# A gated linear attention feeding a SiLU feed-forward: the second token group by plain products, no gap between attention chunks, and an audit held in its written order

## The chip, the core and the metric

The kernel runs on one core of a Trainium2 chip. The core has TensorE (PE: matrix products and transposes, results in PSUM), VectorE (DVE: elementwise work, scans, reductions), ScalarE (ACT: copies out of PSUM, Silu), GpSimd (POOL) and SyncE (SP), whose queue issues all the transfers of this kernel. Each engine works through its own instructions in order; semaphores let one engine wait for another. The metric is the device time of one execution in microseconds; the times below are the median of repeated runs, and the profile is of one execution of its own.

## What is computed

The first part is a recurrent attention with a decay per key channel, for 4 sequences, 8 heads, 768 steps and 48 channels. The second part is a feed-forward network over the 3072 resulting tokens of 384 features, with 2048 hidden features.

```python
# attention, q, k, v, alpha: (4, 8, 768, 48)
for t in range(S):
    state = alpha[:, :, t, :, None] * state + einsum('bhd,bhe->bhde', k[:, :, t], v[:, :, t])
    y[:, :, t] = einsum('bhd,bhde->bhe', q[:, :, t], state)
x = y.transpose(0, 2, 1, 3).reshape(B * S, H * D)      # (3072, 384)
h = x @ w_in                                            # (384, 2048)
out = (h * sigmoid(h)) @ w_out                          # (2048, 384)
```

The inputs reach the kernel as 64-bit floats (the weights) or 32-bit floats; all arithmetic on the chip is in float32.

## The kernel before, in words

**Two paths.** The function `quotients` computes the fast path. It divides by running products of `alpha`, which is only sound if `alpha` and the weights lie in certain bounds, so it also checks its inputs (`audit`, line 576) and hands back a flag. Where the flag says no, `general` computes everything again; on these inputs that branch isn't taken.

**Attention** is cut into 24 chunks of 128 tokens, numbered n, and each goes through four stages:
- `products(n)` (line 612): twelve transposes on PE, a copy on ACT, then on DVE a scan (625), a product (629), a small maximum and a reciprocal (631, 632), a second scan (634) and a product (636).
- `scores(n)` (638): sixteen short matmul records, two masks on DVE (651), four transposes and a copy; for chunks past the first four a decay of the state on DVE (660).
- `values(n)` (665): 32 or 56 narrow matmul records and a copy that lays two chunks side by side as `xt`.
- `states(n)` (686): the state's update, on PE and DVE (699 or 701).

**Feed-forward** works on groups of 512 tokens, four chunks each; there are six groups. Each has two halves h of 256 tokens. It is cut into small "pieces", Python generators that yield after a few instructions.
- `enter_plain(grp, h)` (727) multiplies by w_in plainly: for each pair of the 16 hidden tiles, six products into one PSUM bank, then one Silu. Only group 0 uses it.
- `enter(grp, pair)` (743) computes the same for both halves and half the hidden tiles (a "pair" of "quads" of tiles) by a scheme with fewer products: 20 products for 24, twice, with many additions on DVE (line 770) and copies on ACT (762). It needs eleven sums of tokens (`sums_x`, 709) and 23 sums of w_in blocks (`sums_w`, 531, the list `SUMS_W`), some in place in `w_in`, some in the tile `wx`.
- `leave(grp, h)` (850) multiplies by w_out, in seven steps of eight products of 192 columns (857), with differences of w_out blocks (`t1`, `t2`, `t4` in the tile `wt`, and `b12` in place, `differences`, 539), subtractions between cells of the hidden activations (862) and sums of cells (`side_by_side`, 842). The first one, `leave(0, 0)`, is plain: 64 records of 384 columns (884). Between its four pieces it issues the differences and the first twelve w_in sums; `leave(0, 1)` issues the rest.
- The weights arrive as 64-bit floats. `weights` (544) fetches a block (461, four buffers `bits`) and converts it with one ACT and three DVE instructions (564, 567 to 569): twelve blocks of w_in, sixteen of w_out.

**The order.** Everything is traced in one program order, from which the compiler's scheduler makes the order of each engine: it prefers what was traced first, but lets an instruction go ahead where it expects it to be ready. `tc.keep_in_program_order(i)` pins an instruction behind the one traced before it on the same engine. The loop at line 1022 runs over steps; each step has four slots (`scores` of the chunk before, `products`, `values`, `states`), and behind each slot `fill` (998) adds feed-forward pieces. `begin` (991) leaves two steps without a new chunk after the fourth one. A list `pieces` (968) holds the order: group 0 plain, `leave(0, 0)`, `leave(0, 1)`, `sums_x(1)`, `enter(1, 0)`, `enter(1, 1)`, and from then on `leave(g-1, h)` and `enter(g, h)` alternately (`both`, 960). `fill` deals them out in even shares per slot; `last` keeps a piece back until its chunks are bridged (`values` done). `convert` (953) runs the weight conversions ahead of the pieces that need them.

**The audit.** From step 15 on, every second slot calls `audit` once: it issues a transfer of a piece of `alpha`, w_in or w_out into one buffer and, at once, one or two reductions of it on DVE (602). There are 37 pieces with 65 reductions; those that don't fit into the loop follow in the tail (1035), two feed-forward pieces to each. The flag is computed from them at the end.

**PSUM**: three banks for attention (`ps_a`), three for the products with w_in (`ps_m`), two for those with w_out (`ps_o`). The hidden activations live in six buffers (`gpool`).

Of the kernel before, what the change touches and what calls it, by code (L numbers as in the profile page):

```python
# [355 lines left out]
def quotients(  # L356
# [31 lines left out]
    GB = 4  # L388
# [132 lines left out]
    def combine(to, sa, a, sb, b):  # L521
        if sa == sb == 1:
            dve.tensor_tensor(to, a, b, ALU.add)
        elif sa == 1:
            dve.tensor_tensor(to, a, b, ALU.subtract)
        elif sb == 1:
            dve.tensor_tensor(to, b, a, ALU.subtract)
        else:
            dve.scalar_tensor_tensor(to, a, -1.0, b, ALU.mult, ALU.subtract)

    def sums_w(upto):
        while sums_done[0] < min(upto, len(SUMS_W)):
            to, sa, a, sb, b = SUMS_W[sums_done[0]]
            combine(block_w(to), sa, block_w(a), sb, block_w(b))
            sums_done[0] += 1

    sums_done = [0]

    def differences(i):
        dve.tensor_tensor(t1[:, i], b12[:, i], b11[:, i], ALU.subtract)  # L540
        dve.tensor_tensor(t2[:, i], b22[:, i], t1[:, i], ALU.subtract)
        dve.tensor_tensor(t4[:, i], b21[:, i], t2[:, i], ALU.subtract)
# [33 lines left out]
    def audit():  # L576
# [13 lines left out]
        for src, n, kind in todo:  # L590
            t = late["look"].tile([128, 512, 2], I32, name="bits")
            if kind == 0:
                x = t.rearrange("p n w -> p (n w)")[:, 0:n].bitcast(F32)
                nc.sync.dma_start(x, src)
            else:
                nc.sync.dma_start(t[:, 0:n, :].rearrange("p n w -> p (n w)"), src.bitcast(I32))
                x = t[:, 0:n, 1]
            i = at[kind]
            at[kind] += 1
            for which, op in ((0, ALU.max), (1, ALU.min)):  # L600
                if kind == 1 or which == 0:
                    dve.tensor_reduce(seen[kind][which][:, i : i + 1], x, axis=AX, op=op,  # L602
                                      apply_absolute_value=True)
            yield
# [122 lines left out]
    def enter_plain(grp, h):  # L727

        if h == 0:
            for pair in range(NQ // 2):  # L730
                g_tiles(grp, pair)
        xt = xts[2 * grp + h]
        for f in range(0, NFT, 2):
# [6 lines left out]
            act.activation(gts[grp, h, q // 2][:, i : i + 2, q % 2, :], ps, AF.Silu)  # L740
# [109 lines left out]
    def leave(grp, h):  # L850
# [24 lines left out]
        if grp == h == 0:  # L875
# [3 lines left out]
            for j in range(HF // 2):  # L879
# [16 lines left out]
            for i in range(0, HF, 2):  # L896
                dve.tensor_tensor(b12[:, i : i + 2], b22[:, i : i + 2], b12[:, i : i + 2], ALU.subtract)
# [6 lines left out]
        def done():  # L904
            if grp == 0:
                sums_w(12 + 2 * next(steps) + 2)
# [53 lines left out]
    def both(grp):  # L960
        last = GB * grp + GB
        pieces.append((sums_x(grp), last))
        for h in range(2):
            x, y = leave(grp - 1, h), enter(grp, h)
            for _ in range(7):
                pieces.extend(((x, last), (y, last)))

    pieces = []
    for part, n, last in ((enter_plain(0, 0), HF, 2), (enter_plain(0, 1), HF, 4),
                          (leave(0, 0), HF // 2, 4), (leave(0, 1), 7, 4),  # L970
                          (sums_x(1), 1, 2 * GB), (enter(1, 0), 7, 2 * GB), (enter(1, 1), 7, 2 * GB)):
        pieces += [(part, last)] * n
    ALONE = 15
    START = len(pieces) - ALONE
    for grp in range(2, NG):
        both(grp)
    for h in range(2):
        pieces += [(leave(NG - 1, h), NT)] * 7
# [14 lines left out]
    FIRST = 4  # L993
    SLOTS = 4

    STEADY = (begin[2 * GB - 1] + 1) * SLOTS + 3

    def fill(step, slot):

        if step < FIRST:  # L1000
# [115 lines left out]
```

## Time and profile before

| | us |
|---|---|
| median of three runs (618.08 to 619.08) | 618.42 |
| the profiled execution | 622.89 |
| its span, first to last instruction | 621.1 |
| PE busy | 585.3 |
| PE weight load busy | 521.4 |
| DVE busy | 435.0 |
| ACT busy | 184.7 |
| mean granted TensorE clock | 0.98 of full speed |

A page of the profile lists busy time by engine, the span in 40 equal slices, the transfers, the chain of work that ended last, and the costliest groups of instructions. These are the slices: each digit is the busy share in tenths, and PEclk is the granted clock.

```profile
PE   4889989998999979999999999999999999999996
PEld 3668876697777869989978999999999999999996
DVE  3897999868978798677689577479377365444531
ACT  1335441010335434134233224224233233242200
```

A row of a group of instructions reads: line, engine, operation, output <- input, shape, count | busy time and mean ns of one | idle time of the engine just before them, and what ended it. A row of a stretch gives its bounds and length, then the busy time and the number of instructions of each engine. A row of the timeline gives start, duration, the instruction, and in brackets the idle time before it with its releaser. A row of the chain gives start, duration and the instructions. Busy times of PE overlap, since matmuls are pipelined.

### The profile page before, as it was taken

How to read it: one execution, taken by the hardware profiler on the slowest of the kernel's cores; microseconds unless marked ns; L12 is line 12 of the kernel's file. 1: busy time of each engine (PE TensorE's matmuls, PEld its weight loads, DVE VectorE, ACT ScalarE, POOL GpSimd, SP SyncE). 2: the span in 40 equal slices, each digit the busy share in tenths (PEclk: the TensorE clock that was granted, in tenths of full speed). 3: DMA queues.
4: the chain of work that ended last, by engine and by line, in shares of the span. 5: the costliest groups of instructions: out<-in, count | busy, mean ns of one | idle time of the engine just before them, and what ended most of it. 6: DMA issues, size and time to landing. Idle time of an engine off the chain costs nothing.

```text
span 621.1 us, 10850 instructions
## 1 busy us (share of the span) xinstructions
PE 585.3 (94%) x4450; PEld 521.4 (84%) x4450; DVE 435.0 (70%) x802; ACT 184.7 (30%) x311; POOL 5.2 (1%) x22
## 2 busy tenths in 40 slices
PE   4889989998999979999999999999999999999996
PEld 3668876697777869989978999999999999999996
DVE  3897999868978798677689577479377365444531
ACT  1335441010335434134233224224233233242200
POOL 3000000000000000000000000000000000000000
PEclk9789999997999989999998999999999999999999
DMA  9986964165664524445353233033010000000000
GB/s 208 222 173 199 249 145 86 33 152 155 171 154 85 141 59 92 137 105 115 103 133 72 71 58 52 20 55 55 20 34 1 14 14 6 20 7 13 15 20 30
DMA packets 116169, 54.25 MB, mean 87 GB/s; under 512 B 101648, under 2 KB 107792, under 8 KB 116112
## 3 DMA queue, kind: packets, MB, share of 16 engines
q1 hardware_dynamic: 116112, 53.49, 37.7%
q8 instruction: 36, 0.59, 0.4%
q14 instruction: 21, 0.17, 0.1%
HBM read 48.76 MB, written 4.72 MB: 86 GB/s over the span
## 4 chain that ended last, share of the span: by engine, by line
PE 56%; DVE 27%; DMA 12%; issue 2%; ACT 1%; POOL 1%; DVEq 0%; ACTq 0%; SPq 0%; POOLq 0%
PE ps_o L857 27%; PE ps_m L756 19%; DMA bits<-in_moe_w_out_dram 5%; DMA bits<-in_moe_w_in_dram 5%; DVE seen L602 5%; PE ps_a L680 3%; PE ps_a L620 3%; DVE g L770 3%; DVE p L634 2%; DVE u L625 2%; DMA bits<-in_alpha_dram 2%; PE ps_a L647 2%; DVE u L629 1%; DVE p L636 1%; PE ps_a L655 1%
## 5 line engine op out<-in xcount | busy, mean ns | idle before, releaser
L857 PE MATMUL ps_o<-w_out,g 128*128 128x192 f32 x704 | 126.8, 335 | 0.6 <-DVE o L871 0.6
L857 PEld LDWEIGHTS ps_o<-w_out,g 128*128 128x128 f32 x704 | 118.9, 196 | 3.8 <-issue 1.4
L857 PE MATMUL ps_o<-wt,g 128*128 128x192 f32 x528 | 91.8, 327 | 0.0
L756 PE MATMUL ps_m<-xc,w_in 128*128 128x256 f32 x360 | 88.1, 380 | 1.0 <-DVE g L770 0.9
L857 PEld LDWEIGHTS ps_o<-wt,g 128*128 128x128 f32 x528 | 86.3, 190 | 1.5 <-issue 0.8
L756 PEld LDWEIGHTS ps_m<-xc,w_in 128*128 128x128 f32 x360 | 66.9, 190 | 9.6 <-DVE g L770 1.5
L602 DVE TENSOR_REDUCE seen<-bits 128x1 f32<-128x384 int32 (+2 forms) x65 | 43.2, 689 | 36.9 <-DMA bits<-in_moe_w_out_dram 16.1
L762 ACT COPY g<-ps_m 128x512 f32<-128x512 f32 x80 | 46.8, 588 | 70.2 <-PE ps_m L756 70.2
L767 ACT ACTIVATE g<-g 128x1024 f32<-128x1024 f32 x40 | 41.2, 1054 | 74.1 <-DVE g L770 74.1
L756 PE MATMUL ps_m<-xc,wx 128*128 128x256 f32 x240 | 62.2, 381 | 0.0
L862 DVE TENSOR_TENSOR g<-g 128x512 f32<-128x512 f32 x66 | 45.1, 687 | 17.0 <-PE ps_o L857 16.9
L770 DVE TENSOR_TENSOR g<-ps_m,g 128x512 f32<-128x512 f32 x70 | 46.9, 684 | 6.9 <-PE ps_m L756 5.7
L756 PEld LDWEIGHTS ps_m<-xc,wx 128*128 128x128 f32 x240 | 43.6, 190 | 5.1 <-issue 1.0
L737 PE MATMUL ps_m<-xt,w_in 128*128 128x256 f32 x192 | 45.5, 391 | 0.5 <-DVE w_in L569 0.5
L647 PE MATMUL ps_a<-p,u 48*128 48x128 f32 x384 | 30.2, 297 | 12.5 <-DVE p L636 11.8
L647 PEld LDWEIGHTS ps_a<-p,u 48*128 48x128 f32 x384 | 25.4, 198 | 19.5 <-issue 14.0
L737 PEld LDWEIGHTS ps_m<-xt,w_in 128*128 128x128 f32 x192 | 36.4, 196 | 6.2 <-DVE w_in L569 1.0
L651 DVE TENSOR_TENSOR g<-ps_a,mask 128x512 f32<-128x512 f32 x48 | 31.6, 686 | 11.6 <-PE ps_a L647 11.2
L762 ACT COPY part<-ps_m 128x512 f32<-128x512 f32 x40 | 23.5, 587 | 52.8 <-PE ps_m L756 34.6
L625 DVE TENSOR_TENSOR_SCAN u<-al,one 128x516 f32<-128x516 f32 x24 | 29.5, 1229 | 10.9 <-ACT al L622 10.8
L770 DVE TENSOR_TENSOR g<-g,part 128x512 f32<-128x512 f32 x30 | 20.5, 683 | 17.8 <-ACT part L762 12.8
L756 PE MATMUL ps_m<-xt,w_in 128*128 128x256 f32 x120 | 31.0, 381 | 0.7 <-DVE g L770 0.7
(102 smaller groups left out, 658.4 us busy)
## 6 DMA issues: line engine op xcount, KB each, us to landing
bits<-in_moe_w_in_dram SPq DMA_DIRECT2D x24, 512.0 KB, 3.8
bits<-in_moe_w_out_dram SPq DMA_DIRECT2D x32, 384.0 KB, 3.5
an<-in_alpha_dram SPq DMA_DIRECT2D x24, 192.0 KB, 4.0
kn<-in_k_dram SPq DMA_DIRECT2D x24, 192.0 KB, 4.7
qn<-in_q_dram SPq DMA_DIRECT2D x24, 192.0 KB, 4.7
vn<-in_v_dram SPq DMA_DIRECT2D x24, 192.0 KB, 3.7
bits<-in_alpha_dram SPq DMA_DIRECT2D x9, 512.0 KB, 3.9
out_dram<-o SPq DMA_DIRECT2D x48, 96.0 KB, 1.6
```

The lines of the kernel that those rows point to most:

```text
L602: dve.tensor_reduce(seen[kind][which][:, i : i + 1], x, axis=AX, op=op, apply_absolute_value=True)
L620: pe.transpose(ps[name][:, j, :], c[name][:, 2 * j : 2 * j + 2, :], ident)
L625: dve.tensor_tensor_scan(u[:, end - 1 :: -1], sg[:, end:0:-1], one[:, end:0:-1], 0.0, ALU.mult, ALU.add)
L647: pe.matmul(ps[u][:, j, :], lhsT=c["kp"][r, j, :], rhs=c["qp"][r, j, :], start=True, stop=True)
L651: dve.tensor_tensor(g[:, u], ps[u], mask[:, None, :].to_broadcast([128, NP, C]), ALU.mult)
L737: pe.matmul(ps[:, e, :], lhsT=w_in[:, t, (f + e) * 128 : (f + e + 1) * 128], rhs=xt[:, t, :], start=(t == 0), stop=(t == NKT - 1))
L756: pe.matmul(ps[:, e], lhsT=block_w(w)[:, 2 * pair + e], rhs=block_x(grp, x), start=(first and e == 0), stop=(e == 1), skip_group_check=True)
L762: act.copy(to, ps)
L767: act.activation(x, x, AF.Silu)
L770: dve.tensor_tensor(to, a, b, op)
L857: pe.matmul(ps, lhsT=x, rhs=w[:, i], start=(first and i == 0), stop=(i == HF - 1), skip_group_check=True)
L862: dve.tensor_tensor(cells(grp, h, pair, *to), cells(grp, h, pair, *x), cells(grp, h, pair, *y), ALU.subtract)
```

## The change

Group 1 goes through `enter_plain` too, so `enter`, `sums_x` and the w_in sums start with group 2. `enter_plain` now takes one pair (half the hidden tiles) at a time. The differences, `side_by_side(0, 1, ...)` and `b12` move out of `leave(0, 0)` into the plain pieces of group 1's first pair. `sums_w` works on one pair of quads, so each sum becomes two of half the width: those of the first pair are issued in `leave(0, 1)`, which now alternates with group 1's second pair, those of the second in `leave(1, 0)`, four to a step; they are pinned in program order, as is the first of each set of differences. `begin` and its gap go. The pieces carry weights (`n`), and `fill` deals them out by phases that end at given slots. The conversions are spread anew. In `audit` the generator now yields between a transfer and its reductions, so a call runs the reductions of the piece before and then issues the next transfer, and the reductions are pinned in program order.

```diff
+    def sums_w(pair, upto):
+        r = slice(2 * pair, 2 * pair + 2)
+        while sums_done[pair] < min(upto, len(SUMS_W)):
+            to, sa, a, sb, b = SUMS_W[sums_done[pair]]
+            tc.keep_in_program_order(
+                combine(block_w(to)[:, r], sa, block_w(a)[:, r], sb, block_w(b)[:, r]))
+            sums_done[pair] += 1
...
+    def differences(i):
+        if i < HF // 2:
+            i = slice(2 * i, 2 * i + 2)
+            tc.keep_in_program_order(
+                dve.tensor_tensor(t1[:, i], b12[:, i], b11[:, i], ALU.subtract))
+            dve.tensor_tensor(t2[:, i], b22[:, i], t1[:, i], ALU.subtract)
+            dve.tensor_tensor(t4[:, i], b21[:, i], t2[:, i], ALU.subtract)
         else:
...
+            i -= HF // 2
+            if i % 2 == 0:
+                side_by_side(0, 1, i // 2)
+            i = slice(2 * i, 2 * i + 2)
+            dve.tensor_tensor(b12[:, i], b22[:, i], b12[:, i], ALU.subtract)
...
+            yield
             i = at[kind]
             at[kind] += 1
             for which, op in ((0, ALU.max), (1, ALU.min)):
                 if kind == 1 or which == 0:
...
+                    tc.keep_in_program_order(
+                        dve.tensor_reduce(seen[kind][which][:, i : i + 1], x, axis=AX, op=op,
+                                          apply_absolute_value=True))
...
-    def enter_plain(grp, h):
+    def enter_plain(grp, h, pair):
...
+            if grp == 1 and pair == 0:
+                differences(4 * h + f // 2)
+            if grp > 0 and f % 8 == 6:
+                side_by_side(grp, h, pair)
             yield
...
-                differences(slice(2 * j, 2 * j + 2))
-                if j % 2 == 1:
-                    side_by_side(0, 1, j // 2)
-                sums_w(3 * j + 3)
...
         def done():
-            if grp == 0:
-                sums_w(12 + 2 * next(steps) + 2)
+            if 2 * grp + h in (1, 2):
+                sums_w(2 * grp + h - 1, 4 * next(steps) + 4)
...
+    for h in range(2):
+        for pair in range(2):
+            pieces += [plain(0, h, pair)] * 4
+    pieces += [(leave(0, 0), 24, GB)] * (HF // 2)
+    phases = [len(pieces)]
+    for h in range(2):
+        pieces += [plain(1, h, 0)] * 4
+    both([(leave(0, 1), 12, GB)] * 7, [plain(1, 0, 1)] * 4 + [plain(1, 1, 1)] * 4)
+    phases.append(len(pieces))
+    before = output(1)
     for grp in range(2, NG):
...
+        pieces.append((sums_x(grp), 0, GB * grp + GB))
+        for x, y in zip(before, group(grp)):
+            both(x, y)
+        phases.append(len(pieces))
+        before = output(grp)
+    pieces += before[0] + before[1]
...
-    begin = [n if n < GB else n + 2 for n in range(NT)]
-    STEPS = begin[-1] + 2
...
+    marks = [2 * SLOTS + 2] + [(GB * i + 2 * GB) * SLOTS + 2 for i in range(len(phases))]
...
+        due = a + (b - a) * (at - marks[i] + 1) / (marks[i + 1] - marks[i])
+        if i >= 2 and at % 2:
+            next(audits, None)
+        while work_at[done + 1] <= due and pieces[done][2] <= bridged:
             convert(0, 3 * (done // 2) + 6)
-            convert(1, 2 * done - 8)
+            convert(1, 3 * (done - 6) // 2)
```

By this order `leave(0, 0)` begins at step 6 and ends in step 8, group 1's plain pieces run from there to step 12, and the audit's first call comes at the end of step 12.

More of the change, by code (lines that the diff above doesn't have):

```diff
@@ L725, in bank @@
         return banks[turn[i]].tile([128, 512], F32, name="ps_m")[:, 0:n]
-    def enter_plain(grp, h):
+    def enter_plain(grp, h, pair):
         if h == 0:
-            for pair in range(NQ // 2):
-                g_tiles(grp, pair)
+            g_tiles(grp, pair)
         xt = xts[2 * grp + h]
-        for f in range(0, NFT, 2):
+        for f in range(8 * pair, 8 * pair + 8, 2):
             ps = bank(f // 2 % 3).rearrange("p (e n) -> p e n", e=2)
@@ L1024, in quotients @@
                 ((scores, 1), (products, 0), (values, 1), (states, 1))):
-            if step - lag in begin:
-                n = begin.index(step - lag)
+            n = step - lag
+            if 0 <= n < NT:
                 stage(n)
```

78 lines of the change are left out of this document (26 added, 52 removed).

## The prediction

> **What bounds the kernel now.** I read the page's busy rows first, then the busy time by stretch, then the same stretches for single lines of TensorE (PE) work, then the chain that ended last, then the timeline where PE waits.
>
> ```profile
> span 621.1 us, 10850 instructions
> PE 585.3 (94%) x4450; PEld 521.4 (84%) x4450; DVE 435.0 (70%) x802; ACT 184.7 (30%) x311; POOL 5.2 (1%) x22
> ```
> ```profile
> 0.00:60.00 60.00, 45.85 (x362) 37.02 (x363) 43.89 (x79) 19.63 (x32) 5.16 (x22) 0.91 0.97 200
> 60.00:123.00 63.00, 59.89 (x387) 45.13 (x386) 60.89 (x121) 18.09 (x35) 0.00 (x0) 1.00 0.52 127
> 123.00:227.00 104.00, 93.72 (x869) 81.59 (x869) 83.86 (x144) 32.44 (x55) 0.00 (x0) 0.97 0.58 141
> 227.00:340.00 113.00, 110.19 (x846) 100.66 (x848) 89.67 (x173) 35.29 (x61) 0.00 (x0) 0.97 0.45 104
> ...
> 340.00:616.00 276.00, 275.64 (x1998) 257.00 (x1990) 156.71 (x288) 79.26 (x130) 0.00 (x0) 1.00 0.13 28
> 616.00:621.10 5.10, 0.00 (x0) 0.00 (x0) 0.03 (x1) 0.00 (x0) 0.00 (x0) 0.86 0.09 26
> ```
>
> Columns of a stretch: its length, busy time of PE, PE weight load, VectorE (DVE), ScalarE (ACT), GpSimd, then granted clock, DMA share, GB/s. PE looks 94% busy, but matmuls overlap, so a busy row hides idle time. I count work instead: records times their spacing where PE never waits.
>
> ```profile
> 344.33 2.59 PE ps_m L756 x12
> ...
> 579.17 36.48 PE ps_o L857 x224
> ```
>
> The same stretches for one line of PE work each; first line 756, then 857, 884 and 737 (PE busy and records, weight load):
>
> ```profile
> 123.00:227.00 104.00, 38.11 (x160) 28.95 (x160) 0.97 0.58 141
> ...
> 340.00:616.00 276.00, 105.29 (x456) 85.07 (x456) 1.00 0.13 28
> ```
> ```profile
> 123.00:227.00 104.00, 21.02 (x112) 19.64 (x113) 0.97 0.58 141
> ...
> 340.00:616.00 276.00, 148.25 (x864) 141.33 (x864) 1.00 0.13 28
> ```
> ```profile
> 60.00:123.00 63.00, 21.21 (x64) 11.85 (x64) 1.00 0.52 127
> ```
> ```profile
> 0.00:60.00 60.00, 18.78 (x74) 14.67 (x75) 0.91 0.97 200
> ```
>
> The chain gives 2.59/12 = 0.2158 us per 256-wide record and 36.48/224 = 0.1629 per 192-wide one. Every product leaves two records, a transpose one. Of the 1998 records in 340-616 lines 756 and 857 have 456 and 864, so the other 678 (attention) take (275.64 - 456 x 0.2158 - 864 x 0.1629)/678 = 0.054 each. Line 884's 64 take 21.2; line 737 has 74 of its 192 before 60 and 118 after; line 756 has 800 in all and 857 has 1232, so what 123-227 and 340-616 don't hold of them lies in 227-340. Work and idle by stretch:
> - 0-60: 74 x 0.2158 + 288 x 0.054 = 31.5; idle 28.5.
> - 60-123: 118 x 0.2158 + 21.2 + 205 x 0.054 = 57.7; idle 5.3.
> - 123-227: 160 x 0.2158 + 112 x 0.1629 + 597 x 0.054 = 85.0; idle 19.
> - 227-340: 184 x 0.2158 + 256 x 0.1629 + 406 x 0.054 = 103.3; idle 9.7.
> - 340-616: idle about 0; after it a tail of 5.1.
>
> So PE bounds the kernel from 227, and about 53 us are lost before. To 123 the cover is DVE, 60.89 busy of 63. In 123-227 DVE is neither full nor fast:
>
> ```profile
> 125.12 1.22 DVE L602 TENSOR_REDUCE seen<-bits 128x1 f32<-128x1024 f32 x1 [2.84 <-DMA bits<-in_alpha_dram]
> ...
> 137.01 1.22 DVE L602 TENSOR_REDUCE seen<-bits 128x1 f32<-128x1024 f32 x1 [2.30 <-DMA bits<-in_alpha_dram]
> ...
> 141.91 2.08 PE L647 MATMUL ps_a<-p,u 48*128 48x128 f32 x16 [2.24 <-DVE p L636]
> ```
> ```profile
> L602 DVE TENSOR_REDUCE seen<-bits 128x1 f32<-128x512 int32 (+1 forms) x25 | 21.4, 873 | 17.1 <-DMA bits<-in_moe_w_in_dram 9.5 <-DMA bits<-in_alpha_dram 7.7
> ```
>
> The audit's reduces, written after step 15, were issued from 120 on. DVE sat 2.84 us for one's transfer, attention's scan came late behind it, and PE waited 2.24. Up to 227 the audit took 21.4 us of DVE and left 17.1 idle.
>
> A sentence on a page of the Trainium skill, which nothing below needs: "Perfetto Trace Analysis", Identifying the Most-Contended Engine, calls matmul busy time a bad measure of headroom and weight-load busy time a good one. By the busy rows only 27.5 us are idle to 227; by weight load, full at 257.0/276 = 0.931, 163.7/0.931 leaves 51, and my count says 53, so the trace sides with the page.
>
> **The change part by part.** PE: group 1 takes 96 plain products for 80, two records each: 32 x 0.2158 = **+6.9 us**, surely on the path. DVE:
>
> ```profile
> L770 DVE TENSOR_TENSOR g<-ps_m,g 128x512 f32<-128x512 f32 x70 | 46.9, 684 | 6.9 <-PE ps_m L756 5.7
> ...
> L523 DVE TENSOR_TENSOR xc<-xt 128x256 f32<-128x256 f32 x15 | 6.1, 418 | 0.1
> ...
> L523 DVE TENSOR_TENSOR w_in<-wx,w_in 128x512 f32<-128x512 f32 x4 | 2.6, 682 | 0.0
> ...
> L540 DVE TENSOR_TENSOR wt<-w_out 128x384 f32<-128x384 f32 x4 | 2.2, 546 | 0.0
> ```
> ```profile
> L625 DVE TENSOR_TENSOR_SCAN u<-al,one 128x516 f32<-128x516 f32 x24 | 29.5, 1229 | 10.9 <-ACT al L622 10.8
> L634 DVE TENSOR_TENSOR_SCAN p<-al,inv 128x516 f32<-128x516 f32 x24 | 29.5, 1228 | 0.2
> ...
> L629 DVE TENSOR_TENSOR u<-ps_a,u 128x512 f32<-128x512 f32 x24 | 16.6, 690 | 1.8
> L636 DVE TENSOR_TENSOR p<-ps_a,p 128x512 f32<-128x512 f32 x24 | 16.4, 685 | 1.0 <-DVE p L634 0.6
> ...
> L651 DVE TENSOR_TENSOR g<-ps_a,mask 128x512 f32<-128x512 f32 x48 | 31.6, 686 | 11.6 <-PE ps_a L647 11.2
> ...
> L699 DVE TENSOR_TENSOR st<-ps_a,st 48x192 f32<-48x192 f32 x32 | 11.3, 352 | 2.0 <-PE ps_a L693 1.8
> L660 DVE TENSOR_TENSOR st<-st,u 128x384 f32<-128x384 f32 x20 | 11.0, 550 | 0.0
> ```
>
> Gone: 28 combinations x 0.684 = 19.2 and sums_x(1), 11 x 0.418 = 4.6. The 23 w_in sums (15.7) become 46 of half the width, priced by the 256-wide row: 19.2, now behind the plain products instead of ahead of 123. The 16 differences (16 x 0.55 = 8.8) also leave the stretch before 123. ACT loses 24 copies and 8 Silus and gains 16 Silus; at 30% busy that is worth nothing. One chunk of attention costs DVE 1.23 + 1.23 + 0.69 + 0.69 + 2 x 0.69 + 2 x 0.35 + 0.55 + about 0.3 of small ones = 6.8 and PE 96 x 0.054 = 5.2.
>
> *Start.* The gap's place is taken by chunks 4 and on.
>
> ```profile
> 51.78 0.69 DVE L569 CUSTOM_DVE_ANT_0 w_in<-w_in,up 128x1024 uint16<-128x1024 uint16 x1
> 51.83 15.86 PE L737 MATMUL ps_m<-xt,w_in 128*128 128x256 f32 x72
> ...
> 59.77 0.69 DVE L569 CUSTOM_DVE_ANT_0 w_in<-w_in,up 128x1024 uint16<-128x1024 uint16 x1
> ```
>
> The twelfth conversion of w_in ended at 60.5, behind four chunks on DVE. In the new order the same four chunks and twelve conversions stand ahead of chunk 4, so it ends there again; conversions come in threes, so their transfers queue on SP ahead of chunk loads, and a late one delays this by a few us (DMA share is 0.97 already). Then 24 records follow, to about 65; PE has then done 96 x 0.2158 + 300 x 0.054 = 37: **idle 28**. Bounds 22 (conversions no longer held up) and 33.
>
> *To the end of leave(0, 0).* PE gets two more chunks (+10.4 us of work that leaves the next stretch); DVE loses sums and differences (24.5) and gains two chunks (13.6). It was 97% busy and is about 11 us lighter, so **idle 5**, as now; bounds 2 and 10.
>
> *Group 1 plain, with leave(0, 1).* No audit, no combinations. PE: 192 x 0.2158 + 112 x 0.1629 + four chunks = 80 us; DVE: 27 of attention + 8.8 + six sums of halves x 0.69 = 4.1 + half the w_in sums 9.6 + leave's 6 = 56. In 340-616 DVE at 157/276 left PE no idle time; here it is 0.70. **Idle 3** for 19; bounds 1 and 8. The sums are pinned behind leave's subtractions, which wait for PE; queued behind them are attention's scans, for which the next scores wait. Between them PE has four pieces of 2.6 us, so the cover holds.
>
> *Behind it.* A phase (one enter group, one leave group, four chunks) is 160 x 0.2158 + 224 x 0.1629 + 4 x 5.2 = 92 us of PE. In its first half group 2 gives DVE two chunks 13.6, sums_x 4.6, enter 11, leave 6, w_in sums 9.6 and four audit reduces of 1.22 = 50 against PE's 46: DVE is short for a few us. Later phases carry eight audit pieces and some 77 us of DVE on 92. An audit reduce now stands two of a phase's sixteen slots, 11.5 us, behind its own transfer:
>
> ```profile
> bits<-in_moe_w_out_dram SPq DMA_DIRECT2D x32, 384.0 KB, 3.5
> ```
>
> 3.5 us to landing against 11.5, so DVE shouldn't sit; what is late next is PE itself. The audit's one buffer makes SP wait for the reduce before the next transfer, with chunk loads and output stores queued behind it; a load is issued two chunks ahead of its use, so it has some 20 us of slack. Idle now 9.7 with 89.67 + waits of 113 on DVE: I take **8**; bounds 3 and 18. The checks at the end come behind the last reduce, with L5's 36 us of PE still to run: 0 to 2.
>
> **Sum.** Work now 31.5 + 57.7 + 85.0 + 103.3 + 275.6 = 553, then 560. Idle 28 + 5 + 3 + 8, tail 5.1: 560 + 44 + 5.1 = 609.1 of span, 12 under 621.1. The profiled execution took 622.89 (1.8 around its span), 4.5 above the median of 618.42; taking the 12 from the median gives **606.4 us**.
>
> **The rivals.**
> 1. *DVE relief is worth more.* Idle 25 + 2 + 2 + 3 = 32: span 597, median 594.4. For: DVE sheds 11 us where it is 97% busy, and the waits for the audit's transfers go everywhere. Against: the first 60 us, the largest term, have DMA at 0.97 and don't change.
> 2. *The change doesn't do what it says: the idle time only moves.* Two more chunks per stretch and the sums at group 2's head keep DVE the bound: idle 33 + 6 + 4 + 12 = 55, span 620.1, median 617.4. For: 50 us of DVE against 46. Against: that overrun is short, and before 123 DVE gets lighter.
> 3. *Slower: sums and products take turns.* The sums write w_in and wx in place while group 1's second pair, then group 2's first, read them. If ordering is by tile and not by columns, each of twelve batches of four (4 x 0.418 = 1.7 us) stands between PE's pieces: +20.4, median 626.8; it decides from eight exposed batches (13.6 us), more than the 12 gained. Against: the 72-record run of line 737 went on while other columns of w_in were converted (51.78 to 60.5).
>
> **How the numbers follow.** Forecast 606.4 (0.55; 599 to 613, from moving two of its four idle terms halfway to their bounds), rival 1 (0.2), rival 2 (0.15), rival 3 (0.1). The range, 594 to 618, takes in rivals 1 and 2 and leaves out rival 3 and half of rival 1's tail. About 0.2% (617.2 to 619.7) is what a measurement of this kernel can tell from no change. Faster: 0.55 + 0.2 + 0.07 of rival 2 = 0.82; same 0.06; slower 0.1 + 0.02 = 0.12.
>
> **What would show it.** Line 737 with 384 records and line 756 with 640; line 602 nowhere before group 2 and with nearly no wait for DMA; idle in plain group 1 a few us; first piece of leave(1, 0) near 212. Wrong if L737 or L756 waits for line 523 to 529 (rival 3), if PE's idle time before 65 is under 20 or above 35, or if the audit's reduces still make DVE wait.

## The result and the profile after

| | before | after |
|---|---|---|
| median, us (4 runs each, side by side) | 618.75 (618.08 to 619.38) | 601.39 (601.16 to 603.48) |
| profiled execution, us | 622.89 | 601.16 |
| its span, us | 621.1 | 599.4 |

The ratio is 0.9727, with a 95% interval of 0.9702 to 0.9752. The forecast was 606.4 with a range of 594 to 618, so the direction and the range held, and the gain, 17.4 us, was larger than the 12 forecast.

A part of the gain goes with the clock that TensorE (PE) was granted. The 43 executions of the kernel before that stand beside the experiments run from 615.08 us at a mean granted clock of 0.997 to 622.60 at 0.983; the four of the changed kernel run from 601.16 at 0.996 to 603.48 at 0.991. At 0.996 to 0.997 the two kernels are some 14 us apart (615.1 to 615.7 against 601.2), so about 3 of the 17.4 us go with the clock.

The page of the changed kernel: busy times, the slices of PE and of its clock, and the audit's reduces (now line 616).

```profile
PE 580.2 (97%) x4482; PEld 520.6 (87%) x4482; DVE 421.0 (70%) x786; ACT 171.8 (29%) x295; POOL 5.1 (1%) x22
...
PE   4799999999999999999999999999999999999996
...
PEclk9899999999999999999999999999999999999999
...
L616 DVE TENSOR_REDUCE seen<-bits 128x1 f32<-128x384 int32 (+2 forms) x65 | 42.5, 688 | 5.3 <-DMA bits<-in_moe_w_in_dram 3.0
```

Behind slice 2 PE has no slice under 9 tenths until the tail. The busy time by stretch, columns as in the prediction; the cuts lie where its steps end (end of `leave(0, 0)`, start of `leave(1, 0)`, last product):

```profile
0.00:60.00 60.00, 47.08 (x356) 39.11 (x356) 45.95 (x81) 20.61 (x34) 5.14 (x22) 0.97 0.99 213
60.00:124.10 64.10, 64.10 (x526) 49.12 (x528) 51.04 (x99) 19.59 (x38) 0.00 (x0) 1.00 0.60 139
124.10:208.40 84.30, 84.30 (x745) 75.60 (x745) 50.67 (x101) 17.44 (x33) 0.00 (x0) 1.00 0.25 46
208.40:594.10 385.70, 384.76 (x2866) 356.73 (x2862) 273.01 (x507) 114.16 (x190) 0.00 (x0) 1.00 0.29 74
594.10:599.40 5.30, 0.00 (x0) 0.00 (x0) 0.29 (x1) 0.00 (x0) 0.00 (x0) 0.87 0.08 25
```

The same for the plain product (line 749) alone, and then for the entering products (line 772):

```profile
0.00:60.00 60.00, 22.39 (x96) 0.97 0.99 213
60.00:124.10 64.10, 22.57 (x98) 1.00 0.60 139
124.10:208.40 84.30, 44.02 (x192) 1.00 0.25 46
```
```profile
208.40:594.10 385.70, 148.22 (x640) 1.00 0.29 74
```

So line 749 has 384 records (386 here, since a record that lies across a cut counts in both stretches) and line 772 640, as the change says. With the prediction's prices (0.2158 us for a 256-wide record, 0.1629 for a 192-wide one, 21.2 for `leave(0, 0)`, 0.054 for the rest) the work is 559.6 us over the whole run, 560.7 added up by stretch, and the idle time is:

| stretch | forecast | measured |
|---|---|---|
| start, to 60 | 28 (to about 65) | 25.2 |
| to the end of `leave(0, 0)` | 5 | 2.1 |
| plain group 1 | 3 | 0.7 |
| behind it | 8 | 5.4 |
| tail | 5.1 | 5.3 |

What PE still waits for in the whole run (engine, line, what for; total us, times, longest; the two rows left out are of attention, 0.6 and 0.4); nothing here is a product waiting for a sum of w_in:

```profile
PE ps_a L660 <- DVE p L649: 5.7, 2, 4.4
PE ps_a L633 <- POOL mask L491: 4.2, 1, 4.2
PE ps_a L633 <- DVE g L664: 1.2, 1, 1.2
PE ps_o L873 <- ACT g L783: 0.8, 2, 0.4
PE ps_m L749 <- ACT xt L698: 0.6, 1, 0.6
...
```

### The profile page after: what moved, and what is told of

It reads as the page before. It is cut to its first block, busy times and chain, and to the rows that moved or that the text cites. A ratio compares the mean times of both kernels' runs of the same rounds, so it can differ in the third digit from the quotient of the medians.

```text
span 599.4 us, 10864 instructions
## 1 busy us (share of the span) xinstructions
PE 580.2 (97%) x4482; PEld 520.6 (87%) x4482; DVE 421.0 (70%) x786; ACT 171.8 (29%) x295; POOL 5.1 (1%) x22
## 4 chain that ended last, share of the span: by engine, by line
PE 88%; DVE 8%; ACT 1%; issue 1%; POOL 1%; DVEq 0%; ACTq 0%; POOLq 0%
PE ps_o L873 32%; PE ps_m L772 22%; PE ps_m L749 11%; PE ps_a L693 5%; PE ps_a L633 4%; PE ps_a L660 4%; PE ps_o L900 3%; PE ps_a L706 3%; PE ps_a L668 2%; DVE u L638 1%; DVE g L786 1%; DVE w_in L581 1%; DVE p L647 1%; DVE u L642 1%; DVE w_in L580 1%
## 5 line engine op out<-in xcount | busy, mean ns | idle before, releaser
L749 PE MATMUL ps_m<-xt,w_in 128*128 128x256 f32 x384 | 89.0, 382 | 0.6 <-ACT xt L698 0.6
L749 PEld LDWEIGHTS ps_m<-xt,w_in 128*128 128x128 f32 x384 | 70.7, 190 | 11.1 <-issue 1.0
L772 PE MATMUL ps_m<-xc,w_in 128*128 128x256 f32 x288 | 70.1, 379 | 0.0
L772 PEld LDWEIGHTS ps_m<-xc,w_in 128*128 128x128 f32 x288 | 53.5, 190 | 6.2
L778 ACT COPY g<-ps_m 128x512 f32<-128x512 f32 x64 | 37.5, 586 | 50.2 <-PE ps_m L772 50.2
L772 PE MATMUL ps_m<-xc,wx 128*128 128x256 f32 x192 | 50.1, 383 | 0.0
L783 ACT ACTIVATE g<-g 128x1024 f32<-128x1024 f32 x32 | 33.1, 1055 | 52.2 <-DVE g L786 52.2
L786 DVE TENSOR_TENSOR g<-ps_m,g 128x512 f32<-128x512 f32 x56 | 37.2, 683 | 6.2 <-PE ps_m L772 5.7
L638 DVE TENSOR_TENSOR_SCAN u<-al,one 128x516 f32<-128x516 f32 x24 | 29.5, 1229 | 14.4 <-ACT al L635 14.4
L772 PEld LDWEIGHTS ps_m<-xc,wx 128*128 128x128 f32 x192 | 35.0, 190 | 4.7 <-issue 1.2
L752 ACT ACTIVATE g<-ps_m 128x512 f32<-128x512 f32 x32 | 19.1, 596 | 60.4 <-PE ps_m L749 60.3
L660 PEld LDWEIGHTS ps_a<-p,u 48*128 48x128 f32 x384 | 24.1, 193 | 13.3 <-issue 10.1
L786 DVE TENSOR_TENSOR g<-g,part 128x512 f32<-128x512 f32 x24 | 16.6, 690 | 23.9 <-ACT g L778 14.9
L778 ACT COPY part<-ps_m 128x512 f32<-128x512 f32 x32 | 18.7, 585 | 44.0 <-PE ps_m L772 44.0
```

What stands on the lines that cost most here:

```text
L638: dve.tensor_tensor_scan(u[:, end - 1 :: -1], sg[:, end:0:-1], one[:, end:0:-1], 0.0, ALU.mult, ALU.add)
L660: pe.matmul(ps[u][:, j, :], lhsT=c["kp"][r, j, :], rhs=c["qp"][r, j, :], start=True, stop=True)
L749: pe.matmul(ps[:, e, :], lhsT=w_in[:, t, (f + e) * 128 : (f + e + 1) * 128], rhs=xt[:, t, :], start=(t == 0), stop=(t == NKT - 1))
L772: pe.matmul(ps[:, e], lhsT=block_w(w)[:, 2 * pair + e], rhs=block_x(grp, x), start=(first and e == 0), stop=(e == 1), skip_group_check=True)
L778: act.copy(to, ps)
L783: act.activation(x, x, AF.Silu)
```

## The experiments

The diff has four parts that can be made alone: the audit's order, the missing gap, the plain product of group 1 with its sums behind it, and (in the new schedule; the change names only the conversions, "spread anew") an earlier pace of w_in's conversions and first pieces. All times are medians; ratios are to runs of the kernel before at the same time. Idle time is counted as in the prediction, from the records of each line in each stretch.

| | kernel | us | ratio (95%) | idle to 60 | 60-123 | 123-227 | 227-340 |
|---|---|---|---|---|---|---|---|
| | before | 618.75 | 1 | 28.5 | 5.1 | 18.7 | 9.7 |
| | after | 601.39 | 0.9727 (0.9702-0.9752) | 25.2 | 1.9 | 2.4 | 2.4 |
| 1 | before + audit's order | 601.84 | 0.9711 (0.9674-0.9747) | 26.1 | 5.9 | 4.4 | 4.2 |
| 2 | before + no gap | 620.20 | 1.0012 (0.9990-1.0035) | 30.2 | 4.3 | 16.6 | 9.8 |
| 3 | 1 + no gap | 601.82 | 0.9721 (0.9683-0.9760) | 28.9 | 3.0 | 4.3 | 4.2 |
| 4 | after, audit as before | 613.23 | 0.9884 (0.9844-0.9924) | 25.7 | 3.1 | 7.8 | 12.1 |
| 5 | before + pin only | 601.56 | 0.9722 (0.9676-0.9768) | 28.5 | 5.2 | 5.5 | 3.5 |
| 6 | before + separation only | 617.86 | 0.9997 (0.9972-1.0022) | 26.1 | 6.0 | 18.0 | 5.3 |
| 7 | after, half of group 1 plain | 598.05 | 0.9677 (0.9628-0.9725) | 25.7 | 1.8 | 2.3 | 2.8 |
| 8 | after, old conversion pace | 605.75 | 0.9802 (0.9754-0.9850) | 29.1 | 2.5 | 1.8 | 2.6 |
| 9 | 3 + early pace | 600.97 | 0.9758 (0.9732-0.9784) | 25.9 | 6.3 | 3.6 | 4.2 |
| 10 | 9, w_in sums on GpSimd | 609.59 | 0.9885 (0.9866-0.9905) | 28.0 | 15.0 | 4.6 | 2.2 |
| 11 | after, with the gap | 605.08 | 0.9820 (0.9791-0.9849) | 25.2 | 6.1 | 2.1 | 2.6 |
| 12 | after once more | 601.66 | 0.9735 (0.9697-0.9774) | | | | |

The kernel before itself gave medians between 616.75 and 619.74 beside them, so the ratios carry that spread; the control, run 12, repeated the changed kernel to 0.3 us. Differences between versions below are of the medians and are backed by the idle columns.

Two things must be kept in mind with the idle columns. The profiles of before and of runs 2, 4, 5 and 10 are each the longest execution of their kernel (616.99 us for a median of 613.23 in run 4). And every record is counted at its price at full clock, so a stretch at a lower clock counts as idle too. Read in steps of half a microsecond, the granted clock of these profiles is 1.00 or 0.50 but for the step in which it changes. Two stretches of the kernel before, and what line 857 took in the second:

```profile
142.00:148.00 6.00, 5.12 (x28) 4.86 (x29) 5.55 (x10) 0.59 (x1) 0.00 (x0) 0.50 0.39 108
227.50:230.50 3.00, 3.00 (x11) 3.00 (x11) 2.97 (x8) 0.33 (x1) 0.00 (x0) 0.50 0.02 5
```
```profile
227.04 4.45 PE L857 MATMUL ps_o<-w_out,g 128*128 128x192 f32 x16
```

Sixteen such records are 2.6 us at the price of 0.1629. The profiles of before and of runs 2, 4 and 6, whose reduces aren't pinned, have two or three such stretches each between 120 and 340. Those of the changed kernel and of runs 1, 3, 5, 7, 8, 9, 11 and 12, whose reduces are pinned, have none from 47 us to the tail; run 10, pinned too, has one at 116, where PE had long waits. In the kernel before they last some 13.6 us in 123-340, so up to 6.8 of the 28.4 us counted idle there were lost at half clock and not in waits. That the waits bring the half clock about fits all of these profiles, but no run shows it by itself.

**1 to 4: which part carries the gain.** Run 1 changes only the audit (in run 3 together with run 2's line); run 4 takes this part out of the changed kernel.

```
+            yield
             i = at[kind]
...
-                    dve.tensor_reduce(seen[kind][which][:, i : i + 1], x, axis=AX, op=op,
-                                      apply_absolute_value=True)
-            yield
+                    tc.keep_in_program_order(
+                        dve.tensor_reduce(seen[kind][which][:, i : i + 1], x, axis=AX, op=op,
+                                          apply_absolute_value=True))
```

> The kernel before with only the audit's part of the change: a reduce is issued one slot pair behind its transfer and keeps its written place. Theory A (what was lost in 123-227 came mostly from the reduces that VectorE drew ahead and then held for their transfers, so attention's scans were late): the reduces leave 60-227 altogether, the idle time of 123-227 (19 us) falls to between 5 and 11 us, what stands behind 227 stays near 10 us, and the time falls by 8 to 14 us, to 605-611. Theory B (VectorE's load of the products of group 1 and the w_in sums ahead of them is what loses the time, the audit only fills its gaps): the reduces move to 227-616, PE's idle time of 123-227 stays at 15 us or more, and the time stays within 3 us of the kernel before, 616-621.

Run 2 and the other half of run 3:

```
-    begin = [n if n < GB else n + 2 for n in range(NT)]
+    begin = list(range(NT))
```

> The kernel before with only the gap of two steps in attention taken out; group 1 by products and the audit as before. Theory A: the idle time at the start is set by VectorE and the w_in transfers, which are the same, and the reduces still hold VectorE in the stretch behind the first group, which is now shorter by two steps: 0 to 5 us less, 613-619. Theory B: two more chunks (13.6 us of VectorE) stand ahead of the sums that the products of group 1 wait for, so it is no faster and perhaps slower: 617-628.

> Both the audit's part and no gap, but group 1 still by products with its w_in sums ahead of it (7 us less of work on TensorE than with plain products, 24 us more on VectorE). It tells whether the plain product of group 1 is worth its price. Theory A: with the audit out of the way VectorE has room for the combinations, and this comes within 4 us of the changed kernel on either side, 597-605. Theory B: VectorE is the bound up to group 1's end (some 183 us of its work there with about 12 us of start, 195, against 179 for TensorE), so at least 15 us of idle time remain ahead of group 2 and the time is 606-614, over 5 us slower than the changed kernel.

> The changed kernel with the audit written as before: a reduce is issued in the same slot as its transfer and not kept in its place. Theory A: the reduces are drawn ahead into the stretch of the plain group 1 and wait there for their transfers; line 602's successor shows waits for DMA of 10 us or more, attention's scans come late, and the time rises by 4 to 12 us over the changed kernel, to 605-613. Theory B: VectorE has so little to do in the plain stretch (51 of 84 us) that the waits fall into its idle time: within 2 us of the changed kernel, 600-603.

Measured: 601.84, 620.20, 601.82, 613.23. The audit's order alone (run 1) gives the whole gain, theory A, and more of it than A expected (605 to 611). Taking out the gap alone (run 2) gives nothing, within theory B's range. Without the plain product (run 3, theory A) the kernel is as fast as with it. And the changed kernel loses 11.8 us when its audit goes back (run 4, theory A, just above its 613; 10.1 us between the fastest executions, 611.30 and 601.16). The stretch in question in run 1, all lines, then line 757 (entering) and line 858 (leaving):

```profile
123.00:227.00 104.00, 102.38 (x982) 91.67 (x981) 80.71 (x146) 37.75 (x64) 0.00 (x0) 1.00 0.33 57
227.00:340.00 113.00, 112.67 (x888) 103.54 (x887) 80.32 (x141) 34.81 (x58) 0.00 (x0) 1.00 0.38 90
```
```profile
123.00:227.00 104.00, 42.97 (x184) 1.00 0.33 57
...
```
```profile
123.00:227.00 104.00, 26.44 (x154) 1.00 0.33 57
...
```

Work here is 184 x 0.2158 + 154 x 0.1629 + 644 x 0.054 = 99.6, so 4.4 us of 104 are idle, against 18.7 before, with the same products of group 1 and nearly the same busy time of VectorE (DVE), 80.71 us for 83.86. So that busy time as such was not the trouble; what stood in it was. Before, 20.22 us of it were reduces, which waited another 17.1 us for their transfers; in run 1 one reduce of 0.94 us is left there, beside 79.8 us of other work. No run takes the waits away and leaves the reduces in their early place, so how much their busy time cost and how much their waits did stays open. Without the audit's part (run 4), the reduces make PE wait even in the lighter new schedule. DVE and PE around 200 us of run 4:

```profile
197.94 1.28 DVE L614 TENSOR_REDUCE seen<-bits 128x1 f32<-128x512 int32 x2 [3.04 <-DMA bits<-in_moe_w_in_dram]
...
203.01 1.28 DVE L614 TENSOR_REDUCE seen<-bits 128x1 f32<-128x512 int32 x2 [1.88 <-DMA bits<-in_moe_w_in_dram]
...
204.95 1.12 PE L632 MATMUL ps_a<-ident,an 128*128 128x128 f32 x4 [2.96 <-DVE g L663]
```

DVE sits 3.04 and 1.88 us for two transfers, attention's masked scores (line 663) come late behind them, and PE waits 2.96.

**5 and 6: place or separation.** The audit's part does two things: the reduce is pinned, and it stands one slot pair behind its transfer. Run 5 keeps the first, run 6 the second.

```
-                    dve.tensor_reduce(seen[kind][which][:, i : i + 1], x, axis=AX, op=op,
-                                      apply_absolute_value=True)
+                    tc.keep_in_program_order(
+                        dve.tensor_reduce(seen[kind][which][:, i : i + 1], x, axis=AX, op=op,
+                                          apply_absolute_value=True))
             yield
```

> The kernel before with the audit's reduces kept in their written place, but each still right behind its own transfer. Theory A (what costs is where the reduces stand: drawn ahead into 120-227 and waiting there): they go behind 227, each of the 37 pieces holds VectorE for about 3 us there, some 110 us, which just fits beside 261 us busy in the 380 us behind group 1; the idle time of 123-211 falls to about 5 us as in the first experiment and a part of the gain is given back at the heads of the groups: 605-616. Theory B (the separation from the transfer is the whole of it): the waits only move to a later place where VectorE is as needed, 616-630.

```
+            yield
             i = at[kind]
...
-            yield
```

> The kernel before with each reduce written one slot pair behind its transfer, but not kept in place. Theory A (place): the reduces are still drawn ahead, and the time stays within 4 us of the kernel before, 615-622. Theory B (separation): the reduces find their data landed wherever they stand, and nearly all of the gain comes, 601-606.

Measured: 601.56 and 617.86: the pin is all of it (theory A of run 6; run 5 came out under both of its ranges). Where the reduces ran (line 602 of the kernel before, then line 603 of run 5):

```profile
123.00:227.00 104.00, 20.22 (x24) 0.97 0.58 141
227.00:340.00 113.00, 18.69 (x34) 0.97 0.45 104
340.00:594.00 254.00, 3.12 (x6) 1.00 0.13 28
```
```profile
123.00:227.00 104.00, 1.21 (x1) 1.00 0.34 64
227.00:340.00 113.00, 12.26 (x12) 1.00 0.36 86
340.00:594.00 254.00, 29.09 (x52) 1.00 0.26 69
```

Before, 58 of 65 reduces stood in 123-340; pinned, 52 stand behind 340, where DVE had been busy 149 of 254 us. Run 1 shows how much else DVE has to do in these places once the reduces are away: 79.8 of 104 us in 123-227, 69.1 of 113 in 227-340. My price for run 5 was far off: I counted about 3 us of waiting for each of 37 pieces, 110 us. The page of before has the first of these rows, that of run 5 the second:

```profile
L602 DVE TENSOR_REDUCE seen<-bits 128x1 f32<-128x384 int32 (+2 forms) x65 | 43.2, 689 | 36.9 <-DMA bits<-in_moe_w_out_dram 16.1
```
```profile
L603 DVE TENSOR_REDUCE seen<-bits 128x1 f32<-128x384 int32 (+2 forms) x65 | 42.6, 688 | 23.5 <-DMA bits<-in_moe_w_out_dram 10.8
```

Pinned, the reduces wait 23.5 us in all, all of it behind 227 where DVE had room, and the kernel is as fast as run 1. Drawn ahead they waited 36.9 us and the kernel was 18 us slower; written one slot pair later but still drawn ahead (run 6), they waited 33.4 us and nothing was gained. So the place of such an operation decides, and not its distance from its transfer in the program.

**7: less of group 1 plain.** Half of the plain product is taken back: group 1's second pair goes by products, its w_in sums beside the plain pieces.

```
+                sums_w(1, 12 * h + 3 * (f // 2) + 3)
...
-            if 2 * grp + h in (1, 2):
-                sums_w(2 * grp + h - 1, 4 * next(steps) + 4)
+            if 2 * grp + h == 1:
+                sums_w(0, 4 * next(steps) + 4)
...
-    both([(leave(0, 1), 12, GB)] * 7, [plain(1, 0, 1)] * 4 + [plain(1, 1, 1)] * 4)
+    pieces.append((sums_x(1), 0, 2 * GB))
+    both([(leave(0, 1), 12, GB)] * 7, group(1)[1])
```

> The changed kernel with group 1's first pair of quads made plainly and its second pair by products: the second pair's w_in sums go beside the plain pieces, the first pair's beside leave(0, 1); the sums of x stand between. TensorE has 16 records of 0.2158 us less, 3.5 us; VectorE gets about 24 us more (sums 9.6, combinations 9.6, sums of x 4.6) in a stretch of some 81 us in which it was busy 51. Theory A (VectorE has room for it): 598-600, faster than the changed kernel. Theory B (at 74 of 81 us VectorE's queue makes TensorE wait again between combinations and attention): 601-606.

598.05 us (597.82 to 599.90): theory A, and faster than both kernels. It is 3.3 us faster than the changed one, for 3.5 us of work saved, and all of its times lie under all of the changed kernel's (601.16 to 603.48, and 601.41 to 603.39 in run 12). The plain stretch of run 7:

```profile
124.10:208.40 84.30, 84.30 (x750) 75.82 (x750) 69.45 (x148) 24.50 (x43) 0.00 (x0) 1.00 0.26 46
```

DVE went from 50.67 to 69.45 us there and PE still has no gap: the changed kernel had bought more relief for DVE than it used.

**8 and 9: the pace of the conversions.** Run 8 puts the old pace into the changed kernel, run 9 the new pace into run 3.

```
-    marks = [2 * SLOTS + 2] + [(GB * i + 2 * GB) * SLOTS + 2 for i in range(len(phases))]
+    marks = [4 * SLOTS] + [(GB * i + 2 * GB) * SLOTS + 2 for i in range(len(phases))]
...
-                convert(0, (at - SLOTS) * 3 // (marks[0] - SLOTS) + 1)
+                convert(0, (at - SLOTS + 1) * 6 // (marks[0] - SLOTS))
```

> The changed kernel with the first six w_in conversions spread over steps 1 to 3 and the first pieces from step 4, as in the kernel before. Theory A (the start's idle time came out 2.7 us under the forecast because the twelfth conversion ended at 54.4 and not at 60.5, which the earlier conversions caused): the twelfth ends at 58 to 61 again, the idle time before 65 is 28 to 30 us, and the time is 2 to 5 us above the changed kernel, 603-607. Theory B (the transfers of w_in set the start whatever the order): within 1 us of the changed kernel, 600.5-602.5.

```
-    FIRST = 4
     SLOTS = 4
+    FIRST = 2 * SLOTS + 2
...
-        if step < FIRST:
+        at = step * SLOTS + slot
+        if at < FIRST:
             if step >= 1:
-                convert(0, ((step - 1) * SLOTS + slot + 1) * 6 // ((FIRST - 1) * SLOTS))
+                convert(0, (at - SLOTS) * 3 // (FIRST - SLOTS) + 1)
             return
-        at = step * SLOTS + slot + 1
+        at += 1
         if at <= STEADY:
-            share = START * (at - FIRST * SLOTS) // (STEADY - FIRST * SLOTS)
+            share = START * (at - FIRST) // (STEADY - FIRST)
```

> The third experiment's kernel (audit kept in order, no gap, group 1 by products) with the changed kernel's pace of conversions and first pieces: three conversions and then pieces from step 2, slot 2. Theory A (the earlier pace is worth its 4 us by itself, and the plain product only trades work for idle time): 596-599, faster than the changed kernel. Theory B (VectorE, 58.8 of 60 us busy in 60-120 of the third experiment, is the bound there until group 1's sums are made, so TensorE's earlier start only waits longer behind it; the plain product is what lets the earlier pace pay): within 1.5 us of the third experiment, 600-603.5.

605.75 and 600.97. With plain group 1 the pace is worth 4.4 us (theory A of run 8). By products it is worth nothing clear (theory B of run 9): the median is 0.9 us lower than in run 3, but the ratio to before is higher, 0.9758 for 0.9721. Run 8 beside run 3 (605.75, 601.82) also shows that, without the earlier pace, plain group 1 and its schedule are some 4 us slower than group 1 by products. The last conversion of w_in in the changed kernel, then in run 8:

```profile
53.73 0.69 DVE L581 CUSTOM_DVE_ANT_0 w_in<-w_in,up 128x1024 uint16<-128x1024 uint16 x1
```
```profile
62.50 0.68 DVE L581 CUSTOM_DVE_ANT_0 w_in<-w_in,up 128x1024 uint16<-128x1024 uint16 x1
```

It ends 8.8 us later, and the idle time to 60 goes from 25.2 to 29.1; the granted clock is 0.50 from about 24.5 to 28 in both, so this difference is the pace's. In run 9 it is 25.9 to 60 as well, but 6.3 follow in 60-123, where the sums still fill DVE:

```profile
60.00:123.00 63.00, 58.49 (x419) 43.58 (x418) 57.54 (x114) 15.23 (x31) 0.00 (x0) 1.00 0.44 113
```

**10: the w_in sums on GpSimd.** Run 9 with 21 of the 23 w_in sums issued by GpSimd (the expectation says 22; two of the form -a - b stay on VectorE).

```
-    def combine(to, sa, a, sb, b):
+    def combine(to, sa, a, sb, b, on=dve):
...
-            combine(block_w(to), sa, block_w(a), sb, block_w(b))
+            combine(block_w(to), sa, block_w(a), sb, block_w(b), gps)
```

> The ninth experiment's kernel with 22 of the 23 whole w_in sums on GpSimd, which is idle there (x22 instructions in all of the kernel before): 22 x 0.684 = 15.0 us less for VectorE ahead of group 1. Theory A (VectorE's load ahead of group 1 is the bound of the versions by products): idle time to 123 falls by several us and the time by 3 to 8 us under the ninth experiment. Theory B (a sum takes GpSimd so long that the products of group 1 wait for it, or it slows VectorE's operations down): as slow as the ninth experiment or slower, 602 or more.

609.59, within theory B's range. Groups of VectorE in 97-123 of run 10: a scan, one of the two remaining w_in sums, a difference, and an operation on a PSUM tile; then PE's longest wait:

```profile
L626 DVE TENSOR_TENSOR_SCAN u<-al,one 128x516 f32<-128x516 f32 x1 | 2.3, 2290 | 0.0
...
L529 DVE SCALAR_TENSOR_TENSOR wx<-w_in,wx 128x512 f32<-128x512 f32 x1 | 1.7, 1733 | 7.4 <-POOL w_in L527 7.4
L541 DVE TENSOR_TENSOR wt<-w_out,wt 128x384 f32<-128x384 f32 x1 | 1.5, 1546 | 0.0
...
L630 DVE TENSOR_TENSOR u<-ps_a,u 128x512 f32<-128x512 f32 x1 | 0.7, 678 | 0.0
```
```profile
PE ps_a L694 <- DVE u L630: 6.9, 2, 5.8
```

The sum left on VectorE waited 7.4 us for GpSimd, attention's operations were queued behind it (line 630 among them), and PE waited for those. Idle time in 60-123 is 15.0. VectorE's own operations were slowed too (the last section has them), as theory B had it; a version with all 23 sums on GpSimd was not run.

**11: the gap put back into the changed kernel.**

```
-    STEPS = NT + 1
+    begin = [n if n < GB else n + 2 for n in range(NT)]
+    STEPS = begin[-1] + 2
...
-    marks = [2 * SLOTS + 2] + [(GB * i + 2 * GB) * SLOTS + 2 for i in range(len(phases))]
+    marks = [2 * SLOTS + 2] + [(GB * i + 2 * GB + 2) * SLOTS + 2 for i in range(len(phases))]
...
-            n = step - lag
-            if 0 <= n < NT:
+            if step - lag in begin:
+                n = begin.index(step - lag)
```

> The changed kernel with the two-step gap in attention put back behind chunk 3, all marks two steps later. Theory A (the gap itself was worth next to nothing, as the second and third experiments had it with group 1 by products: VectorE's work fills it either way): within 2 us of the changed kernel, 599.5-603.5. Theory B (with VectorE lighter, the two chunks that stand in the gap's place are cover that TensorE now lacks, 10 us of its work): 604-611.

605.08, theory B: 3.7 us slower, about all of it in 60-123 (6.1 idle for 1.9). DVE is not full there:

```profile
60.00:123.00 63.00, 60.21 (x482) 47.05 (x481) 46.78 (x90) 18.91 (x37) 0.00 (x0) 1.00 0.57 132
```

46.78 of 63 us, where run 9 has 57.54. So with DVE full the two chunks bring no cover (run 3 equals run 1), and with DVE light they do; that its load is the reason is argued from these two rows.

**12: a control.**

> The changed kernel itself once more, as a control: the fourth, seventh, eighth and eleventh experiments are each held against its 601.39 from another call. Theory A (its time does not depend on the call, so that 3 us between calls mean something): median 600.5-602.5 and the profile's idle time to 60 again 24 to 27 us. Theory B (calls differ by several us): a median outside 599.5-603.5, and then the differences of 3 to 4 us of the seventh, eighth and eleventh experiments rest on their profiles alone.

601.66, and 25.7 us idle to 60: theory A.

## Why the prediction came out as it did

- **What bounds the kernel.** Right: PE from group 2 on, and some 53 us lost before it. The work came out as forecast (560, counted 559.6), the 6.9 us of plain products among it; but it is a count of records at the prediction's own prices and not a measured time. What the count called idle was in part half clock, which the prediction's rows show (0.91 in 0-60, 0.97 in 123-340) and its sum did not use.
- **Start, 28 forecast, 25.2 measured.** The step "the same four chunks and twelve conversions stand ahead of chunk 4, so it ends there again" failed: the twelfth conversion ended at 54.4, not 60.5. I had read that conversions come in threes, but not that the first pieces, which pull the next three each, begin at step 2 and not at step 4. With the old pace (run 8) the idle time to 60 is 29.1, about what I had put down.
- **To `leave(0, 0)`, plain group 1, behind it: 5, 3 and 8 forecast, 2.1, 0.7 and 5.4 measured.** The directions were right; each came out 2.3 to 2.9 us under its value, the first and the last inside their bounds (2 to 10, 3 to 18), plain group 1 just below its own (1 to 8).
- **What the sum said about causes was wrong.** The step that failed is "No audit, no combinations", where I gave both as reasons for 3 in place of 19 us of idle time: the second was not needed. Run 1 shows that the audit's order alone takes 18.7 to 4.4 in 123-227 and 9.7 to 4.2 in 227-340 with all combinations in place. The rest of the change adds 32 records, 6.9 us of work, and the span goes from 599.7 to 599.4: it takes some 7 us of idle time off and pays the same in work. Without the audit's part it is worth 6.5 us (run 4 against 619.74 beside it), on top of it nothing. So that the forecast's range held is in part luck: the sum credited relief of VectorE and the missing gap with a gain that the audit's order brings alone.
- **From span to median.** The forecast of the span, 609.1, was 9.7 us too high; that of the median only 5.0. I had taken 12 off the median of before, though the terms came from a profiled execution 4.5 us above it, the longest on record, at a mean granted clock of 0.980. That excess belonged into the terms. In before and in runs 1, 5 and 6 VectorE does the same operations in the same order to 59 us. Idle time to 60 is 28.5 us in before and run 5, whose clock was 0.50 for some 10 us there, and 26.1 in runs 1 and 6, whose clock was 1.00. So 2.4 us of the start that I carried over whole were the clock's, and two errors cancelled half.
- **The rivals.** Rival 1 (DVE relief is worth more, idle 32 and the tail) had the idle sum nearly right, 32 for 33.4, for half the reason: not DVE's lighter load but its order. Rival 2 (the idle time only moves) is out by that sum, which it put at 55; rival 3 (sums and products take turns) by the waits list: no product waits on lines 523 to 528.
- **The signs named.** No reduce before group 2 and nearly no wait for DMA: yes, the first reduce came at 231 and all of them waited 5.3 us. First piece of `leave(1, 0)` near 212: it came at about 208.

Not tried: what sets the 25 us at the start with the early pace, a split of the small idle terms behind 60 below what runs 1, 8 and 11 give, and how the 18 us of the audit's order divide into the reduces' busy time, their waits and the half clock.

## What to carry to other kernels

Before giving an engine less work, look at what stands at the head of its queue: an operation with slack of its own (here a check on inputs) that waits for a transfer holds everything behind it. Pinning it to a later place was worth 18 us. On top of that, 15 us less of busy time on VectorE (436.3 in run 1, 421.0 after), bought with 6.9 us of TensorE work, was worth nothing. Test each part of a change alone and all but one: parts that relieve the same wait don't add up (17.9 and 6.5 us alone, 17.4 together), and half of a part may do (run 7). Take a sum's terms and its end figure from the same execution, or from two, since one start can be 2 us longer than the next when the granted clock differs.

## What the runs showed of the hardware

- GpSimd slowed VectorE. In 97-123 of run 10 a scan took 2.29 us, a difference of SBUF tiles 1.55 and an operation with one operand in PSUM 0.68 (rows above). The first row below is of run 10 and shows GpSimd busy 19.84 of 20 us (the fifth pair); behind it stand the same groups of 97-123 in run 9, without GpSimd:

```profile
100.00:120.00 20.00, 14.22 (x103) 9.16 (x102) 9.03 (x8) 1.07 (x2) 19.84 (x15) 0.90 0.17 30
```
```profile
L626 DVE TENSOR_TENSOR_SCAN u<-al,one 128x516 f32<-128x516 f32 x1 | 1.2, 1230 | 0.0
...
L630 DVE TENSOR_TENSOR u<-ps_a,u 128x512 f32<-128x512 f32 x1 | 0.7, 689 | 0.0
...
L541 DVE TENSOR_TENSOR wt<-w_out,wt 128x384 f32<-128x384 f32 x1 | 0.6, 555 | 0.0
```

  The scan took nearly twice and the difference nearly three times as long, and the third is unchanged. The Trainium skill, "SBUF — State Buffer", Who interferes with whom, says that a DVE instruction with two SBUF inputs contends with a GpSimd instruction that reads SBUF, and that one with at most one such input, outside the 2-port modes, doesn't. These three rows agree with it. Two other groups of the same stretch do not follow from it so simply:

```profile
L661 DVE TENSOR_TENSOR st<-st,u 128x384 f32<-128x384 f32 x1 | 0.5, 545 | 0.0
L632 DVE TENSOR_SCALAR least<-u 128x4 f32<-128x4 f32 x1 | 0.5, 516 | 0.0
```
```profile
L661 DVE TENSOR_TENSOR st<-st,u 128x384 f32<-128x384 f32 x1 | 0.6, 556 | 0.0
...
L632 DVE TENSOR_SCALAR least<-u 128x4 f32<-128x4 f32 x1 | 0.2, 169 | 0.0
```

  Line 661, with two inputs in SBUF (one of them a column repeated), took as long in run 10 (the first pair) as in run 9, and line 632, with one, three times as long; each is a single instruction, and no run shows why. A 128x512 sum took GpSimd 1.25 to 2.19 us where VectorE took 0.67 to 0.70 in run 9.
- The granted clock is one of two values, read finely enough. The 160 records of 20-40 us took 14.72 us of PE in run 1 and 16.83 in run 5. The mean granted clock of these 20 us was 1.00 and 0.83; in steps of half a microsecond run 5 has 0.50 from about 22.5 to 29.5 and 1.00 beside it.
